# An attention-and-expert kernel whose first part runs its operations in another order, with seven squares on GpSimd

## The chip, the cores and the metric

The kernel runs on one core of a Trainium2 chip. The metric is the device time of one execution in microseconds (us); before the change the median of three runs is 1042.24 us (1042.18 to 1042.42). The core has a matrix engine (PE), a vector engine (DVE), an activation engine (ACT), GpSimd (POOL), and a queue on SyncE (SP) that issues nearly all transfers. Each engine takes its instructions strictly in the order in which the program has them, so an instruction that waits holds back all behind it on that engine.

## The reference

Random-feature attention over 8 batches, 8 heads, 576 tokens and 64 dimensions with 128 features, then a gated product with three weight matrices (512 to 1536, twice, and back):

```python
def phi(x):
    proj = np.einsum('bhsd,md->bhsm', x, omega)
    sq = np.sum(x * x, axis=-1, keepdims=True) / 2.0
    h = proj - sq
    h = h - np.max(h, axis=-1, keepdims=True)
    return np.exp(h) / np.sqrt(m)
q_p, k_p = (phi(q_s), phi(k_s))
kv = np.einsum('bhsm,bhsd->bhmd', k_p, v)
z = np.sum(k_p, axis=2)
num = np.einsum('bhsm,bhmd->bhsd', q_p, kv)
den = np.einsum('bhsm,bhm->bhs', q_p, z)[..., None] + 1e-06
...
a = x @ w_a
b = x @ w_b
return (a * b @ w_out).astype(np.float32)
```

`q_s` and `k_s` are q and k times D^-1/4. What the change touches is `sq`: the sum of squares of each key and query, which goes into the bias of the exponential.

## The kernel before

**Staging.** The work is cut into 32 units, each a batch and a pair of heads (`_b_h` in names: `natq_0_2` belongs to batch 0, head pair 2). The four pairs of batch 0 go through the functions `pair` and `tok_tail`, those of later batches through `shifted`, `divide`, `turn` and `num`. For a pair of batch 0 the steps are: project keys and queries on PE into PSUM (`ppk`, `ppq`); take maxima on DVE (`sm`, L627) and make the biases (L634, L635) with the sums of squares; exponentials on ACT (L640, 16 instructions for a pair: `hk`, `hq`); `kv` on PE (`pkv`), copied by ACT to `kvz`; three transposes of the query features on PE (`pq`), copied to `qT` by ACT or DVE; numerators and denominators on PE (`pn`, L994); the division on DVE (`rd`, `x32t`, `tails`); a transpose back (`px`, `pt`); and the result `x_0_h` in two parts, a high one that ACT casts and a low one that DVE gets by subtraction.

**Weights.** The inputs are in 64 bits. A tile `raw` of 128x512 such numbers is made into one of 32 bits by two ACT instructions (L446, L448) and a merge on DVE (L450); then a high part is cast (L396 on ACT or L398 on DVE) and a low part subtracted on DVE (L404). The tiles come in the order `raw0` = first tile of w_a (`wa0`), `raw1` = `wb0`, `raw2` = `wo0`, and so on in threes. A product of two such split numbers takes three matrix instructions.

**The blocks.** For each of 12 slices of the 1536 columns a block of 512 tokens needs 12 matrix instructions for `pa` and 12 for `pb` (L1250), a product of the two on DVE (`a`, L1258), its split into `ghl`, and 12 instructions for the output `o` (L1060). The first instruction of block 0 is `pa` of slice 0; it needs `wa0` and `x_0_0`. Blocks 2 and later use a scheme with seven products in place of eight (L1343), on sums of the weights that are made on DVE and ACT while block 1 runs. Attention units of later batches run between the blocks' instructions.

**Sums of squares.** For most units keys and queries also come in natural layout (`natk`, `natq`, at batch ends `natee`; 128x512 each). `square_sums` squares such a tile in place on ACT (L560, with the scale folded in) and sums it on DVE (L562) into `sq`. Later, POOL adds up key features (L802).

**What sets the order.** Every operation is recorded with its buffers and a cost; a planner (`Graph.plan`) plays the engines with these costs and gives one list of 5,637 operations in order of planned start. The program is emitted in that order, so each engine's and each queue's instructions stand as the list has them. Where an operation may run on more than one engine, the planner picks.

## Time and profile before

| | |
|---|---|
| median of three runs | 1042.24 us |
| the profiled execution's own time | 1041.62 us |
| its span, first to last instruction | 1039.8 us |
| PE busy | 1024.4 us (99%) |
| DVE busy | 887.3 us (85%) |
| ACT busy | 598.4 us (58%) |
| POOL busy | 114.0 us (11%) |
| bytes read and written | 255.52 MB and 57.18 MB |

A busy PE is one with a matrix instruction under way; its ends are modelled, and an instruction that is slow or held back inside the pipeline counts as busy. So what PE loses is read from its idle time, from its rate (how long twelve equal instructions take) and from the granted clock, stretch by stretch. A row of the timeline gives the start, the duration, engine, line, operation, names, shapes and count, and in brackets idle time before it and what ended that.

### The profile page before, as it was taken

The page shows a single profiled execution, that of the slowest core. Times are in us where ns is not written, and L with a number is a line of the kernel's source. Part 1 is how long each engine was busy: PE and PEld are TensorE (multiplying, and loading weights), DVE is VectorE, ACT ScalarE, POOL GpSimd, SP SyncE. Part 2 cuts the span into 40 slices and gives each one's busy share as a digit, 9 for nine tenths or more (in the row PEclk, how much of TensorE's full clock was granted, in tenths as well). Part 3 has the DMA queues.
Part 4 walks back from the last instruction along what each step waited for, and adds up shares of the span by engine and source line. Part 5 has one row for each costly group of instructions (what it writes and reads, how often), then busy time and mean ns, then how long its engine had stood idle before and what let it go on. Part 6 is the DMA issues. An engine that isn't in the chain of part 4 may idle for free.

```text
span 1039.8 us, 26266 instructions
## 1 busy us (share of the span) xinstructions
PE 1024.4 (99%) x9902; PEld 897.0 (86%) x9902; DVE 887.3 (85%) x2212; ACT 598.4 (58%) x1656; POOL 114.0 (11%) x181
## 2 busy tenths in 40 slices
PE   9899999999999999999999999999999999999998
PEld 7677777777788888988888888888899899999998
DVE  6999999899999888878887978888876579998766
ACT  8997798677665665566565656665454123332211
POOL 0032211120111111111101111111110000000000
PEclk9999999999999999999999999999999999999999
DMA  9877879989899998999989988989888888899981
GB/s 352 308 281 239 285 242 307 304 331 317 298 349 363 307 317 294 315 330 313 306 275 351 310 300 296 339 303 309 272 288 268 268 320 313 318 344 341 371 303 47
DMA packets 123665, 314.44 MB, mean 302 GB/s; under 512 B 17681, under 2 KB 40977, under 8 KB 123537
## 3 DMA queue, kind: packets, MB, share of 16 engines
q1 hardware_dynamic: 122656, 312.10, 86.5%
q8 instruction: 78, 1.28, 0.5%
q10 hardware_dynamic: 880, 0.66, 0.2%
q14 instruction: 51, 0.41, 0.1%
HBM read 255.52 MB, written 57.18 MB: 301 GB/s over the span
## 4 chain that ended last, share of the span: by engine, by line
PE 79%; DVE 8%; ACT 1%; issue 1%; DVEq 0%; ACTq 0%
PE p L1343 39%; PE o L1060 19%; PE o_P L1130 5%; PE pa L1250 3%; PE pb L1250 3%; PE pkv L849 3%; PE pm L917 2%; PE ppk L594 1%; PE p L594 1%; DVE sm L627 1%; DVE c L1353 1%; PE p L1130 1%; DVE zero L868 1%; PE ppk L574 1%; PE ppke L574 1%
## 5 line engine op out<-in xcount | busy, mean ns | idle before, releaser
L1353 DVE TENSOR_TENSOR c<-p,c 128x512 f32<-128x512 f32 (+1 forms) x336 | 207.7, 618 | 67.9 <-PE p L1343 59.4
L1060 PE MATMUL o<-wo,ghl 128*128 128x512 f32 x1008 | 258.5, 397 | 0.4 <-DVE ghl L404 0.3
L1060 PEld LDWEIGHTS o<-wo,ghl 128*128 128x128 f32 x1008 | 181.0, 188 | 39.9 <-issue 4.7
L1343 PE MATMUL p<-Sa,t 128*128 128x256 f32 x1008 | 132.6, 281 | 0.0
L1343 PEld LDWEIGHTS p<-Sa,t 128*128 128x128 f32 x1008 | 124.6, 188 | 0.4 <-issue 0.2
L802 POOL TENSOR_TENSOR z<-hk 128x256 f32<-128x256 f32 x56 | 44.5, 795 | 607.7 <-ACT hk L640 431.3
L396 ACT CAST ghl<-c 128x512 fp32r<-128x512 f32 (+1 forms) x75 | 42.5, 579 | 100.5 <-DVE c L1403 80.9
L878 ACT ACTIVATE hq<-hq,dn 128x128 f32<-128x128 f32 x224 | 71.1, 392 | 29.1 <-DVE dn L874 28.9
L868 DVE CUSTOM_DVE_ANT_0 zero<-hq,zb 128x128 bf16<-128x128 f32 x224 | 79.5, 355 | 4.9
L1250 PE MATMUL pa<-x,wa 128*128 128x512 f32 x288 | 75.9, 406 | 3.6 <-ACT wa L396 2.0
L1343 PE MATMUL p<-Sb,bq 128*128 128x256 f32 x504 | 74.1, 283 | 0.0
L1343 PE MATMUL p<-x,t 128*128 128x256 f32 x504 | 74.0, 282 | 0.0
L1250 PE MATMUL pb<-x,wb 128*128 128x512 f32 x288 | 73.3, 398 | 0.4 <-DVE a L1258 0.4
L1343 PE MATMUL p<-Sb,t 128*128 128x256 f32 x504 | 73.5, 282 | 0.0
L396 ACT COPY c<-p 128x256 f32<-128x256 f32 x84 | 31.3, 372 | 73.0 <-PE p L1343 62.3
L1343 PEld LDWEIGHTS p<-x,wa 128*128 128x128 f32 x504 | 64.9, 188 | 7.2 <-DVE c L1353 3.7
L1343 PE MATMUL p<-x,wa 128*128 128x256 f32 x504 | 68.2, 283 | 2.0 <-DVE c L1353 1.0
L1250 PEld LDWEIGHTS pa<-x,wa 128*128 128x128 f32 x288 | 53.6, 191 | 19.0 <-ACT a L396 2.2
L640 ACT ACTIVATE hq<-hq,sm 128x128 f32<-128x128 f32 x192 | 65.4, 392 | 7.4 <-DVE sm L635 6.0
L1343 PEld LDWEIGHTS p<-x,wb 128*128 128x128 f32 x504 | 64.6, 188 | 3.8 <-DVE c L1353 0.6
L1343 PE MATMUL p<-x,wb 128*128 128x256 f32 x504 | 67.7, 282 | 0.1
L1343 PEld LDWEIGHTS p<-x,t 128*128 128x128 f32 x504 | 65.8, 189 | 1.6 <-DVE c L1353 0.4
(209 smaller groups left out, 2019.6 us busy)
## 6 DMA issues: line engine op xcount, KB each, us to landing
t<-td SPq DMA_DIRECT2D x168, 512.0 KB
...
```

The costliest lines, as they stand in the source:

```text
L396: nc.scalar.copy(o(), i())
L574: nc.tensor.matmul(pps[w].ap[half, c * M:c * M + M], x()[rows, c * P + D * t:c * P + D * t + D], om.ap[rows], start=True, stop=True)
L640: g.op({"ACT": 392}, lambda e, c=c, w=w, to=to, at=at: nc.scalar.activation(to.ap[:, at + c], src[w](c), AF.Exp, scale=SC, bias=sm.ap[:, 2 ...
L802: g.op({"POOL": pool2(n)}, lambda e: nc.gpsimd.tensor_tensor(o(), a(), c(), op=ALU.add), r=r, w=w, alloc=list(al), prio=pri, deps=zload[-1 ...
L849: nc.tensor.matmul(pkv.ap[D * j + d:D * j + d + Q, 0:M], vb.ap[:, vc, d:d + Q], c(), start=(n == 0), stop=(n == 4))
L868: g.op({"DVE": 413}, lambda e, c=c, j=j, rr=rr, qc=qc: nc.vector.tensor_tensor_reduce(out=junk.ap[rr], in0=qc(), in1=zb.ap[rr, j], scale=1 ...
L878: g.op({"ACT": 392}, lambda e, c=c, src=src: nc.scalar.activation(hq.ap[:, c], src(), AF.Copy, scale=dn.ap[:, c:c + 1]), r=[sd, (dn, None) ...
L1060: nc.tensor.matmul(po.ap[:], ghl.ap[:, gi, t * P:(t + 1) * P], wo.ap[:, wi], start=(n == 0 and i == 0), stop=(n == NF - 1 and i == 2))
L1130: nc.tensor.matmul(pb.ap[:, t], A[0](ai)[:, t * P:(t + 1) * P], W[0](wi), start=begin and t == j == 0, stop=stop and t == 1 and j == 2)
L1250: nc.tensor.matmul(pb.ap[:], wt.ap[:, wi, c], xs[c].at(xi), start=(c == 0 and i == 0), stop=(c == NC4 - 1 and i == 2))
L1343: nc.tensor.matmul(pb.ap[:, half], wcol(wi, c), xc(xi, c), start=n == 0, stop=n == 5)
L1353: g.op({"DVE": dve(n)}, lambda e: nc.vector.tensor_tensor(c4.ap[:, o], pb.ap[:, half], y(), op=ALU.add), r=[*((pb, k) for k in range(half. ...
```

## The change

The planner's list is kept up to the last step, and then a fixed table rearranges it. `OTHER` gives 44 operations another engine: 7 from ACT to POOL (squares: `natq_0_1`, `natk_0_2`, `natq_0_2`, `natk_0_3`, `natq_0_3`, `natkk_1_0`, `natee_1_0`), 18 from ACT to DVE and 19 from DVE to ACT (casts and copies, of weights, of `ghl`, of `qT` and of outputs). `AFTER` puts 1,409 operations of the first 2,308 of the list behind another one. From 355 us of the profile before on, every engine's order is what it was; the buffers' places in memory are the same throughout.

A square on POOL is a plain product of the tile with itself, without the scale. The scale (SQ2) is applied by a small POOL instruction to the eight sums of each partition, after DVE's sum; the biases on DVE then wait for POOL.

```diff
+OTHER = ((61,"POOL"),(130,"POOL"),(133,"POOL"),(136,"DVE"),(139,"POOL"),(142,"POOL"),(211,"POOL"),(237,"POOL"),(259,"ACT"),(269,"DVE"),
...
+AFTER = ((6,4),(0,8),(20,16),(14,20),(23,14),(19,23),(13,19),(27,31),(35,27),(25,34),(33,36),(32,39),(48,32),(45,40),(51,45),
...
+def arranged(order):
+    for i, e in OTHER:
+        order[i].eng = {e: 0}
+    moved = {i for i, _ in AFTER}
+    follow = {}
+    for i, j in AFTER:
+        follow[j] = i
+    got = []
+    def put(i):
+        while i is not None:
+            got.append(i)
+            i = follow.pop(i, None)
+    put(follow.pop(-1, None))
+    for i in range(len(order)):
+        if i not in moved:
+            put(i)
+    return [order[i] for i in got]
...
-            g.op({"ACT": act(n * D)}, lambda e, nat=nat: nc.scalar.activation(nat.ap[:], nat.ap[:], AF.Square, scale=SQ),
-                 r=[(nat, None)], w=[(nat, None)], prio=pr, margin=0 if b < 2 else CFG["LOAD"])
-            g.op({"DVE": dve(n * D)}, lambda e, nat=nat, o=o: nc.vector.tensor_reduce(o(), nat.ap[:], axis=X, op=ALU.add),
-                 r=[(nat, None)], w=[(sq, part)], alloc=[sq] if part in (0, None) else [], prio=pr)
+            s = g.op({"ACT": act(n * D)}, lambda e, nat=nat: nc.scalar.activation(nat.ap[:], nat.ap[:], AF.Square, scale=SQ) if e == "ACT" else
+                     nc.gpsimd.tensor_tensor(nat.ap[:], nat.ap[:], nat.ap[:], op=ALU.mult),
+                     r=[(nat, None)], w=[(nat, None)], prio=pr, margin=0 if b < 2 else CFG["LOAD"])
+            def total(e, nat=nat, o=o, s=s):
+                nc.vector.tensor_reduce(o(), nat.ap[:], axis=X, op=ALU.add)
+                if "POOL" in s.eng:
+                    nc.gpsimd.tensor_scalar(o(), o(), SQ2, 0.0, op0=ALU.mult, op1=ALU.add)
+            g.op({"DVE": dve(n * D)}, total, r=[(nat, None)], w=[(sq, part)], alloc=[sq] if part in (0, None) else [], prio=pr)
...
-    order = g.plan()
+    order = arranged(g.plan())
```

Line numbers in the changed kernel are higher by 25 in the helpers and by 30 behind `square_sums`. Three places show how the rows move.

First, SP's queue of loads, from its thirteenth transfer on. Before:

```order
L407 DMA X_0_30_171<-in_kqt_dram 128x1024
L407 DMA natk_0_3_173<-in_kqn_dram 128x512
L407 DMA natq_0_3_175<-in_kqn_dram 128x512
L407 DMA v_0_3_177<-in_vx_dram 128x660
L407 DMA Xe_1_0_202<-in_kqtt_dram 128x512
L407 DMA Xk_1_0_204<-in_kqt_dram 128x512
L407 DMA X_1_0_206<-in_kqt_dram 128x1024
L407 DMA raw0_216<-in_wab_dram 128x512
L407 DMA raw1_218<-in_wab_dram 128x512
```

Now:

```order
L432 DMA natq_0_3_168<-in_kqn_dram 128x512
L432 DMA Xe_1_0_191<-in_kqtt_dram 128x512
L432 DMA raw1_197<-in_wab_dram 128x512
L432 DMA raw0_199<-in_wab_dram 128x512
L432 DMA v_0_3_201<-in_vx_dram 128x660
L432 DMA raw5_327<-in_wout_dram 128x512
L432 DMA natkk_1_0_382<-in_kqn_dram 128x512
L432 DMA X_0_30_384<-in_kqt_dram 128x1024
```

The first two weight tiles stand earlier (`raw0` sixteenth instead of twentieth, `raw1` fifteenth instead of twenty-first), and `X_0_30`, the keys and queries of head pair 3, later (twentieth instead of thirteenth).

Second, ACT and DVE where the fourth head pair of batch 0 ends and block 0 begins. ACT before:

```order
L396 COPY qT_0_3_740<-pq_0_31_784 128x384
L446 ACTIVATE raw1_218<-raw1_218 128x512
L448 ACTIVATE raw1_218<-raw1_218 128x512
L448 ACTIVATE raw0_216<-raw0_216 128x512
L396 COPY kvz_0_3_791<-pkv_0_3_790 128x132
L446 ACTIVATE raw0_216<-raw0_216 128x512
L396 CAST x_0_2_829<-px_0_2_828 128x512
L396 COPY xts0_571<-pt_0_2_835 128x64
L446 ACTIVATE raw2_223<-raw2_223 128x512
L448 ACTIVATE raw2_223<-raw2_223 128x512
L448 ACTIVATE raw3_267<-raw3_267 128x512
L396 CAST wa0_878<-raw0_216 128x512
```

ACT now:

```order
L471 ACTIVATE raw4_523<-raw4_523 128x512
L473 ACTIVATE raw4_523<-raw4_523 128x512
L473 ACTIVATE raw3_517<-raw3_517 128x512
L421 COPY qT_0_3_738<-pq_0_31_777 128x384
L421 COPY kvz_0_3_782<-pkv_0_3_781 128x132
L473 ACTIVATE raw2_519<-raw2_519 128x512
L421 COPY qT_0_3_738<-pq_0_32_805 128x384
L421 CAST x_0_2_842<-px_0_2_841 128x512
```

DVE before:

```order
L450 SCALAR_TENSOR_TENSOR raw1_218<-raw1_218 128x512
L398 COPY qT_0_3_740<-pq_0_32_838 128x384
L404 TENSOR_TENSOR x_0_2_829<-px_0_2_828,x_0_2_829 128x512
L450 SCALAR_TENSOR_TENSOR raw0_216<-raw0_216 128x512
L450 SCALAR_TENSOR_TENSOR raw2_223<-raw2_223 128x512
L398 CAST wb0_880<-raw1_218 128x512
L999 TENSOR_SCALAR rd_0_31_865<-pn_0_31_864 128x5
L404 TENSOR_TENSOR wa0_878<-raw0_216,wa0_878 128x512
L404 TENSOR_TENSOR wb0_880<-raw1_218,wb0_880 128x512
```

DVE now:

```order
L423 CAST wa0_835<-raw0_199 128x512
L1032 TENSOR_TENSOR x32t_0_2_754<-pn_0_21_765,rd_0_21_766 128x4x64
L1036 TENSOR_SCALAR tails_0_2_731<-pn_0_20_752,rd_0_20_753 64x64
L1032 TENSOR_TENSOR x32t_0_2_754<-pn_0_20_752,rd_0_20_753 128x4x64
L423 COPY qT_0_3_738<-pq_0_30_737 128x384
L429 TENSOR_TENSOR wb0_810<-raw1_197,wb0_810 128x512
L429 TENSOR_TENSOR wa0_835<-raw0_199,wa0_835 128x512
L475 SCALAR_TENSOR_TENSOR raw4_523<-raw4_523 128x512
L1029 TENSOR_SCALAR rd_0_30_859<-pn_0_30_858 128x5
L1029 TENSOR_SCALAR rd_0_31_875<-pn_0_31_874 128x5
L429 TENSOR_TENSOR x_0_2_842<-px_0_2_841,x_0_2_842 128x512
```

ACT's conversions of `raw0` and `raw1` have moved ahead, between the exponentials of head pairs 2 and 3; the high parts of `wa0` and `wb0` are both cast by DVE, and the low parts follow right behind the first copy to `qT_0_3`.

Third, POOL's first compute instructions, which are all new (before, POOL does nothing but clear tiles until it adds up key features, L802):

```order
L586 TENSOR_TENSOR natq_0_2_154<-natq_0_2_154 128x512
L586 TENSOR_TENSOR natq_0_1_152<-natq_0_1_152 128x512
L592 TENSOR_SCALAR sq_0_1_302<-sq_0_1_302 128x8
L586 TENSOR_TENSOR natk_0_3_158<-natk_0_3_158 128x512
L586 TENSOR_TENSOR natk_0_2_160<-natk_0_2_160 128x512
L586 TENSOR_TENSOR natq_0_3_168<-natq_0_3_168 128x512
L1015 MEMSET tails_0_0_469 64x128
L592 TENSOR_SCALAR sq_0_3_471<-sq_0_3_471 128x8
L592 TENSOR_SCALAR sq_0_2_474<-sq_0_2_474 128x8 x2
L592 TENSOR_SCALAR sq_0_3_471<-sq_0_3_471 128x8
L586 TENSOR_TENSOR natkk_1_0_382<-natkk_1_0_382 128x512
L586 TENSOR_TENSOR natee_1_0_386<-natee_1_0_386 128x512
```

The squares of pair 3 and pair 2 stand between the small scalings, which wait for DVE's sums.

More of the change, by code (lines that the diff above doesn't have):

```diff
@@ L42 @@
 CFG = dict(PORT=0.5, EDF=("DVE", "ACT", "POOL"), STEP=15000, LOOK=60000, NOISE=(200, 600), CHOSEN=((858009,0,387055,152612,0,0,0,715321,0,0,680034,0,0,0,0,780129,689749,0,892332,0,0,84647,0,0,0,0,0,0,0,0,0,0,0,0,0,0,0,0,0,0,0,0,0,0,0,0,0,0,0,0,0,0,0,0,0,0,0,0,0,0,0,0,0,0,0,0,0,0,0,0),), ZS=800, ZB=(300, 1600, 3600), ZD=(300, 1600, 3100), HQ=(1100, 2600, 3600), BACK2=(300, 1100, 2600), TW=(), XL=["v0", "v1", "Xt0", "ht2", "hq0"], OWR=["raw0", "raw1"], ONE=((7, 1),), SAFE=500, OWN=16, OWNU=(), HOLD=1000, TG=1, G4=4, WAIT=150, RAW=600, FAST=(0, 1, 2, 3), JOIN0=False, WARM=8, HROOM=["w0", "u1", "w1", "u2", "w2", "u3"], H=3, TURN=(7,), BACK=1500, AT=2, GATES=(-4, -1, 2, 5), SQPE=4, MARGIN=1200, LOAD=1100, SUMS=1000, NATS=(1, 2, 3), CONV=(28000, 2600))
+OTHER = ((61,"POOL"),(130,"POOL"),(133,"POOL"),(136,"DVE"),(139,"POOL"),(142,"POOL"),(211,"POOL"),(237,"POOL"),(259,"ACT"),(269,"DVE"),(297,"ACT"),(352,"ACT"),(355,"DVE"),(423,"DVE"),(447,"ACT"),(449,"ACT"),(475,"ACT"),(494,"ACT"),(560,"ACT"),(562,"ACT"),(638,"ACT"),(674,"ACT"),(708,"ACT"),(720,"ACT"),(740,"DVE"),(794,"DVE"),(868,"DVE"),(976,"DVE"),(1006,"DVE"),(1142,"DVE"),(1152,"DVE"),(1168,"ACT"),(1224,"DVE"),(1255,"ACT"),(1331,"DVE"),(1403,"ACT"),(1498,"ACT"),(1597,"DVE"),(1679,"DVE"),(1848,"ACT"),(1892,"DVE"),(1950,"ACT"),(2035,"DVE"),(2049,"DVE"),)
```

1 line of the change is left out of this document (added).

## The prediction

> **What bounds the kernel now.** I read the page first, then PE's waits, the windows, and the timeline around the longest wait.
>
> ```profile
> PE 1024.4 (99%) x9902; PEld 897.0 (86%) x9902; DVE 887.3 (85%) x2212; ACT 598.4 (58%) x1656; POOL 114.0 (11%) x181
> 50.00:150.00 100.00, 98.59 (x847) 75.27 (x847) 98.93 (x258) 86.63 (x228) 23.55 (x30) 1.00 0.80 273
> 300.00:450.00 150.00, 149.00 (x1554) 132.48 (x1552) 127.35 (x339) 87.53 (x255) 17.99 (x30) 1.00 0.93 325
> ```
>
> The last two rows are windows: length, busy time of PE, weight load, DVE, ACT and POOL, granted clock, share and rate of the DMA engines. PE is the bound: busy 99% of the span. Another order can win only where PE idles or runs slowly before it becomes the old order again. Windows of 5 us show where that is:
>
> ```profile
> 0.00:5.00 5.00, 4.00 (x36) 1.82 (x40) 0.11 (x1) 2.12 (x3) 0.99 (x10) 1.00 0.57 182
> 5.00:10.00 5.00, 5.00 (x100) 4.54 (x92) 4.07 (x9) 3.61 (x11) 0.00 (x0) 1.00 0.97 343
> 10.00:15.00 5.00, 5.00 (x116) 4.20 (x115) 4.82 (x14) 4.97 (x18) 0.00 (x0) 1.00 1.04 408
> 15.00:20.00 5.00, 4.39 (x93) 3.39 (x94) 3.28 (x12) 5.00 (x20) 0.00 (x0) 1.00 1.05 410
> 20.00:25.00 5.00, 4.57 (x116) 3.84 (x114) 4.90 (x12) 5.00 (x17) 0.20 (x1) 1.00 1.03 412
> 25.00:30.00 5.00, 4.27 (x116) 3.68 (x109) 4.62 (x16) 4.82 (x19) 0.00 (x0) 1.00 1.04 402
> 30.00:35.00 5.00, 4.74 (x95) 4.01 (x95) 4.51 (x15) 5.00 (x19) 0.20 (x1) 1.00 1.02 408
> 35.00:40.00 5.00, 2.69 (x58) 2.25 (x54) 4.46 (x8) 5.00 (x12) 0.20 (x1) 1.00 0.87 342
> 40.00:45.00 5.00, 4.49 (x12) 3.24 (x13) 4.88 (x14) 5.00 (x10) 0.00 (x0) 0.66 0.57 209
> ```
>
> From 10 to 45 us ACT is full, DVE is not (3.28 of 5 at 15), POOL does nothing, and PE waits. From 40 to 45 the granted clock is 0.66. PE's waits name the work, first from 37 to 52 us, then from 52 to 450:
>
> ```profile
> PE pa L1250 <- ACT wa L396: 2.0, 1, 2.0
> PE pn L994 <- ACT kvz L396: 0.8, 1, 0.8
> PE pa L1250 <- ACT a L396: 0.7, 1, 0.7
> ```
>
> ```profile
> PE p L1343 <- ACT hk L396: 0.8, 1, 0.8
> PE pa L1250 <- ACT a L396: 0.7, 1, 0.7
> PE pb L1250 <- DVE a L1258: 0.4, 1, 0.4
> PE o L1060 <- DVE ghl L404: 0.3, 1, 0.3
> ```
>
> So 3.5 us of idle PE in 15 us and, with two rows of 0.2 left out, 2.6 us in the next 400. Before 37 us the longest wait that is not the program's start is this one, two more of 0.5 and 0.4 behind it:
>
> ```profile
> PE px L1013 <- DVE x32t L1002: 0.7, 1, 0.7
> ```
>
> The first stretch on the timeline of PE, and one of full rate:
>
> ```profile
> 37.12 1.39 PE L994 MATMUL pn<-kvz,qT 128*64 128x66 f32 x40 [0.82 <-ACT kvz L396]
> 40.51 3.95 PE L1250 MATMUL pa<-x,wa 128*128 128x512 f32 x9 [2.00 <-ACT wa L396]
> 44.27 2.50 PE L1250 MATMUL pb<-x,wb 128*128 128x512 f32 x9
> 50.71 1.53 PE L1250 MATMUL pa<-x,wa 128*128 128x512 f32 x5 [0.69 <-ACT a L396]
> 138.09 2.92 PE L1250 MATMUL pa<-x,wa 128*128 128x512 f32 x12
> ```
>
> Nine instructions take 3.76 us from 40.51 to 44.27; at full rate twelve take 2.76 (138.09 to 140.85), so nine 2.07. The low clock costs 1.7 us there, and 0.2 in the next nine.
>
> **The change part by part.** I follow one milestone: the start of `pa` of slice 1, at 50.71. Behind it PE hardly waits, so what is gained there stays, if the others keep up.
>
> (1) *The squares leave ACT.*
>
> ```profile
> 19.65 0.78 ACT L560 ACTIVATE natk<-natk 128x512 f32<-128x512 f32 x1
> 20.17 0.78 ACT L560 ACTIVATE natq<-natq 128x512 f32<-128x512 f32 x1
> 34.88 0.93 ACT L446 ACTIVATE raw<-raw 128x512 f32<-128x512 f32 x1
> 35.46 1.46 ACT L448 ACTIVATE raw<-raw 128x512 int32<-128x512 uint32 x2
> 36.57 0.50 ACT L396 COPY kvz<-pkv 128x132 f32<-128x132 f32 x1
> ```
>
> Starts lie 0.52 us apart for squares and 0.55 for conversions: that is what one holds of ACT. All seven squares stand ahead of `kvz_0_3` (36.57), the copy for which `pn` of pair 3 waits: 7 x 0.52 = 3.6. A third of `qT_0_1` goes to DVE, 0.4 more. Ahead of `kvz_0_3` come instead four conversions more than before (both of `raw4`, one of `raw3`, the second of `raw0`): 4 x 0.55 = 2.2. Net, ACT is there 1.8 earlier.
>
> (2) *DVE takes over as second bound.*
>
> ```profile
> 32.53 0.55 DVE L398 COPY qT<-pq 128x384 f32<-128x384 f32 x1
> 38.77 1.33 DVE L450 SCALAR_TENSOR_TENSOR raw<-raw 128x512 int32<-128x512 int32 x2
> 40.02 0.42 DVE L398 CAST wb<-raw 128x512 fp32r<-128x512 f32 x1
> 40.49 0.69 DVE L404 TENSOR_TENSOR wa<-raw,wa 128x512 fp32r<-128x512 f32 x1
> ```
>
> Ahead of the first copy to `qT_0_3` (32.53), which `pn` needs too, now stand two merges and two sums of squares at about 0.6, two casts at 0.35, and the divisions of pair 2, 2.3: 5.4 us more. In the windows from 5 to 35 us DVE is busy 26.2 of 30, and its instructions start a little ahead of the last one's end, so some 4.4 of idle time lie there to be filled: the copy comes between 33.5, all of it used, and 37.9, none. I take 35.4, a little nearer to the first, since the merges and sums wait for loads and for POOL alone, not for PE. `pn` starts 0.6 behind it, at 36.0 instead of 37.12, and ACT is there by then: **-1.1** (bounds -3 and +1).
>
> (3) *The wait for wa.* Right behind that copy DVE makes the low parts of `wb0` and `wa0`, whose raw tiles are converted long before: 0.5 + 0.6 + 0.7 = 1.8 behind the copy's start, while `pn` ends 2.0 behind it (0.6 + 1.4). The wait of 2.0 shrinks to about 0.3: **-1.7** (bounds -2.0 and 0).
>
> (4) *The clock.* The one drop of the granted clock inside the program follows the one idle stretch of 2.0 us; waits of 0.7 and 0.8 did not bring it. With 0.3 it should not come: **-1.9** (bounds -1.9 and 0).
>
> (5) *What is late next.* `px_0_3` stands fourth after `pa`'s begin; DVE divides its input behind the low parts, a merge, a subtraction and four small ones, 4.5 behind the copy; PE arrives at 2.3 + 3 x 0.69 = 4.4: with a semaphore's delay **+0.3** (0 to +2). The wait at 50.71 goes, as `wa1` and `x_0_3` have less ahead of them on both engines: **-0.8** (-0.8 to 0).
>
> (6) *The loads.* By the windows' rates 0.9 MB have moved by 5 us, 2.6 by 10, 4.7 by 15, 6.7 by 20. In the new order 4.9 and 5.4 MB end with `raw1` and `raw0` (15.5 and 17 us; 6.9 and 7.4 before), and 7.0 with `X_0_30`, near 21 us. PE took it up at 22.84:
>
> ```profile
> 22.84 0.32 PE L574 MATMUL ppk<-om,X 64*64 64x128 f32 x1
> ```
>
> That costs nothing unless PE runs ahead there by over 1 us.
>
> (7) *The squares on POOL.*
>
> ```profile
> L802 POOL TENSOR_TENSOR z<-hk x56: 724/742/1093, 52.7 to 771.5; 128x256 f32<-128x256 f32 x56
> L802 POOL TENSOR_TENSOR zs<-z x56: 450/476/1143, 53.7 to 772.7; 128x128 f32<-128x128 f32 x56
> 15.49 0.17 DVE L635 SCALAR_TENSOR_TENSOR sm<-sq,sm 128x8 f32<-128x8 f32 x1
> 69.20 1.23 DVE L404 TENSOR_TENSOR wo<-raw,wo 128x512 fp32r<-128x512 f32 x1
> L802 POOLq MODIFY_POOL_CONFIG x2: 4/4/4, 36.2 to 36.2; - x2
> ```
>
> Minimum, median and longest, in ns: 128 columns more cost 266 by the medians, so 512 take 742 + 2 x 266 = 1.27 us (estimate; bounds 1.0 and 2.3, twice the longest). The first tile is the sixth transfer, 1.6 MB: by the rates 7 us, and with a transfer's delay I take 8.9. Four squares in a row end at 14.0; the scaling that stands between the second and the third waits for DVE's sum and makes that about 15. DVE asks for the fourth when it has made pair 1's biases, at 15.66: hidden, by little. The other scalings stand off the path. The price lies on DVE: its subtraction at 69.20 took 1.23, not 0.69, with POOL at work beside it. In the first 35 us five such instructions may meet a square, 5 x 0.54 = 2.7 at most, much of it in idle time: **+0.4** (0 to +2.7).
>
> (8) *The order from 52 to 450 us.* Here only in-order queues count. With each operation at its kind's spacing I compared work ahead of PE's instruction and ahead of its producer, old and new. The producers that end the waits of the table above gain 1 to 3 us of lead (`wa6`, `ghl` of slices 4 and 11, the first sums of block 2); near 337 to 375 some lose about 1. I take **-1.0** of the 2.6 (bounds -2.6 and +3). DVE's work ahead at 300 us differs by only 0.3, ACT's is less. After 450 nothing changes.
>
> Sum: -1.1 - 1.7 - 1.9 + 0.3 - 0.8 + 0.4 - 1.0 = -5.8. The profiled execution took 1041.62 us, 1.8 around its span of 1039.8, which the order does not touch: 1035.8. It stands 0.6 below the median of the runs, so **1036.4**.
>
> **Rivals.** (a) *More*: PE's waits before 37 us, 1.6, go too, `px_0_3` waits for nothing, and all of (8) comes: another 1.6 + 0.3 + 1.6, about 1033. For it: ACT was full there. Against: so is DVE now.
>
> (b) *The clock still drops*: DVE late by 1 us keeps a wait ahead of `pa`: 1.9 and 1.0 come back, 1039.3.
>
> (c) *DVE is already the bound*: busy 98.93 of 100 from 50 to 150. If that were full, a PE that starts 5 us earlier runs into it, and with 0.3 less work ahead at 300 us all is lost: 1042. Against: an instruction of 0.69 starts 0.60 to 0.65 after the last (38.77, two in 1.33), so 12% of busy is overlap, and PE waited for DVE only 0.9 of 400 us.
>
> (d) *Slower: POOL's queue is late.* The fourth square ends at about 10 + 4X for a square of X; from X = 1.5 on, DVE stands at the sum of `natk_0_2`, with the divisions of pair 0 and the maxima of pair 2 behind it, and PE waits for these. Each 0.1 more costs 0.4; at 3.5 it is 8, so 1036.4 + 8 = 1044.4. Against: no L802 row comes near. The same happens if POOL's first operation has to wait for its code: before, POOL was prepared for L802 at 36.2 us, 16 us ahead of its first use, so no row prices it. The Trainium skill (GPSIMD Engine Reference, Instruction dispatch) has a first call of a newly loaded routine cost some 6 us without a trace row; begun at 1.6 us that ends ahead of 8.9, begun at the call it would come to 1036.4 + 6 = 1042.4.
>
> **How the numbers follow.** Forecast 0.45, with 1034.5 to 1038.5 as its own range; (a) 0.18; (b) 0.17; (c), or gains and late queues in balance, 0.12; (d) 0.08. A measurement here tells 0.2%, 2.1 us, from no change. Faster: 0.45 + 0.18 + 0.17 = 0.80; same 0.12; slower 0.08. The range reaches over (a) and (b) and stops ahead of (c): 1031.5 to 1040.9, the lower end for bounds that add up below (a).
>
> **What would show it.** Right: `pn` of pair 3 near 36.0, `pa` behind it with under 0.7 of idle time, granted clock 1.00 from 35 to 45, `pa` of slice 1 near 45.5, the same lead at 150 and 450 us; squares on POOL of 1.2 to 1.5 us, each over before DVE's sum asks for it. Wrong: a clock under 1 there, DVE idle for POOL at 15 to 17 us, or a lead that shrinks between 50 and 300.

## The result, and the profile after

The changed kernel takes 1055.02 us (1053.06 to 1056.23, four runs) beside 1042.26 us (1042.18 to 1042.42): a ratio of 1.012, 95% interval 1.0103 to 1.0138. It is 12.8 us slower. The forecast was 1036.4.

The profiled execution has a span of 1053.6 us, 13.8 longer. By 50 us it has gained nearly what was forecast, though not step by step as forecast (below). Windows of 5 us of the changed kernel, with the columns as in the prediction:

```profile
35.00:40.00 5.00, 4.50 (x91) 3.90 (x92) 4.92 (x17) 5.00 (x11) 0.20 (x1) 1.00 0.77 263
40.00:45.00 5.00, 5.00 (x52) 3.86 (x51) 4.91 (x13) 4.84 (x11) 0.00 (x0) 1.00 0.99 378
45.00:50.00 5.00, 5.00 (x24) 4.01 (x22) 4.96 (x12) 5.00 (x14) 0.81 (x1) 1.00 1.03 411
```

PE is busy 14.5 of 15 us, 12.2 before, and the granted clock is 1.00. On the timeline of PE the block begins without a wait, and slice 1 begins at 46.60 instead of 50.71:

```profile
37.98 1.39 PE L1024 MATMUL pn<-kvz,qT 128*64 128x66 f32 x40
39.30 1.66 PE L1280 MATMUL pa<-x,wa 128*128 128x512 f32 x6
...
46.60 2.89 PE L1280 MATMUL pa<-x,wa 128*128 128x512 f32 x12
```

The loss lies behind it. PE's waits from 60 to 460 us, the five longest in total:

```profile
PE pb L1280 <- DVE a L1288: 3.3, 3, 1.7
PE p L1373 <- DVE c L1383: 1.8, 2, 1.4
PE o L1090 <- DVE ghl L429: 1.5, 3, 0.9
PE o L1090 <- ACT osb L421: 1.3, 1, 1.3
PE p L1373 <- ACT c L421: 0.9, 2, 0.5
```

Before, all waits there came to 2.6 us; these five are 8.8, and PE is busy for 387.4 of these 400 us, 397.1 before. Around the longest of them, windows of the changed kernel show PE at 3.27 of 5, and the clock falls behind it:

```profile
170.00:175.00 5.00, 3.27 (x23) 1.90 (x16) 4.93 (x12) 3.55 (x11) 2.71 (x4) 0.90 0.16 64
175.00:180.00 5.00, 5.00 (x65) 3.55 (x68) 4.64 (x19) 2.23 (x4) 0.00 (x0) 0.76 0.51 129
```

A low clock as the prediction found it at 41 us comes here instead, once: by these two windows it costs some 1.5 us (0.10 of 3.27 and 0.24 of 5.00). The DMA share of 0.16 shows a second thing: few transfers are under way there.

The orders differ, so the times of single instructions say little. For the comparisons below I gave every operation of PE (and of DVE) the spacing that its kind reaches in the fastest tenth of the kernel before, added these up, and asked when each kernel had done as much work as the kernel before at a given time. The lead in us (minus: behind), for the runs told below; the column is the time in the kernel before. Where the orders differ most the count depends on what is taken as one kind: with kinds by names and shapes some entries at 200 and 300 us move by up to 5 us, those at 180 and from 360 on by at most 0.5.

```
                            60     100    140    180    200    300    360    450   1000
changed kernel        PE   4.3     3.4    1.0   -3.1   -4.8   -7.3  -11.9  -12.1  -13.9
                      DVE  2.0     0.8   -3.0   -6.9   -4.9  -10.9  -11.2
e1 early              PE   5.0     1.1    1.2    1.1    1.1    1.1    0.9    0.7   -1.2
e2 late               PE  -0.5    -0.6   -2.3   -4.7   -7.1   -8.8  -13.4  -13.4  -13.5
                      DVE -0.5    -3.2   -6.3   -8.4   -7.9  -12.4  -12.8
e3 half               PE   5.0     4.0    1.4   -1.2   -9.7   -9.4   -9.9  -10.1  -12.1
e18 late from 180     PE  -0.5    -0.5   -0.5   -0.5   -3.6   -6.1  -10.6  -10.6  -10.8
e10 before, bunched   PE  -0.2    -0.6   -1.9   -2.6   -2.6   -4.6   -4.8   -4.9   -4.6
e11 new, no adds      PE   4.2     4.5    4.9    4.8    2.5    2.0   -1.8   -2.0   -3.8
e12 before, no adds   PE  -0.7    -0.1    0.6    0.6    0.6    1.8    1.8    1.9    1.7
e14 new, small dn     PE   4.4     4.7    3.2    2.0   -0.4   -0.9   -5.1   -5.4   -7.2
e16 early, no adds    PE   4.2     1.9    3.1    3.2    3.1    4.5    4.3    4.2    2.5
e17 early, addresses  PE   4.8     1.4    1.6    1.6    1.6    1.7    1.7    1.7    1.7
```

So the 13.8 us (13.9 by this count) are 4.3 gained by 60 us, 16.4 lost from there to 450, and 1.8 lost between 450 and 1000, where the order of every engine is the same as before.

### The profile page after: what moved, and what is told of

It reads as the page before. It is cut to its first block, busy times and chain, and to the rows that moved or that the text cites. A ratio compares the mean times of both kernels' runs of the same rounds, so it can differ in the third digit from the quotient of the medians.

```text
span 1053.6 us, 26259 instructions
## 1 busy us (share of the span) xinstructions
PE 1030.6 (98%) x9902; PEld 900.1 (85%) x9902; DVE 894.7 (85%) x2211; ACT 595.6 (57%) x1650; POOL 123.9 (12%) x195
## 4 chain that ended last, share of the span: by engine, by line
PE 70%; DVE 16%; ACT 6%; DMA 5%; issue 2%; SPq 1%; POOL 0%; DVEq 0%; ACTq 0%; POOLq 0%
PE p L1373 38%; PE o L1090 16%; PE o_P L1160 4%; PE pkv L879 2%; DVE zero L898 2%; DVE sm L657 2%; PE pm L947 2%; PE ppk L624 1%; PE p L624 1%; DVE raw L475 1%; DVE c L1383 1%; ACT hq L908 1%; DVE sq L590 1%; ACT hk L670 1%; ACT hq L670 1%
## 5 line engine op out<-in xcount | busy, mean ns | idle before, releaser
L1090 PE MATMUL o<-wo,ghl 128*128 128x512 f32 x1008 | 265.1, 398 | 3.0 <-DVE ghl L429 1.5
L832 POOL TENSOR_TENSOR z<-hk 128x256 f32<-128x256 f32 x56 | 46.9, 838 | 617.3 <-ACT hk L670 455.5
L908 ACT ACTIVATE hq<-hq,dn 128x128 f32<-128x128 f32 x224 | 72.7, 393 | 34.0 <-DVE dn L904 33.8
L898 DVE CUSTOM_DVE_ANT_0 zero<-hq,zb 128x128 bf16<-128x128 f32 x224 | 81.8, 365 | 9.1 <-DMA zb<-zdr 2.4
L1280 PE MATMUL pb<-x,wb 128*128 128x512 f32 x288 | 79.0, 400 | 3.3 <-DVE a L1288 3.3
L1280 PE MATMUL pa<-x,wa 128*128 128x512 f32 x288 | 79.2, 402 | 0.6 <-DVE wa L429 0.6
L670 ACT ACTIVATE hk<-hk,sm 128x128 f32<-128x128 f32 x184 | 63.6, 393 | 9.5 <-DVE sm L665 4.6
L1280 PEld LDWEIGHTS pb<-x,wb 128*128 128x128 f32 x288 | 53.0, 188 | 17.9 <-DVE a L1288 5.0
```

What stands on the lines that cost most here:

```text
L670: g.op({"ACT": 392}, lambda e, c=c, w=w, to=to, at=at: nc.scalar.activation(to.ap[:, at + c], src[w](c), AF.Exp, scale=SC, bias=sm.ap[:, 2 ...
L832: g.op({"POOL": pool2(n)}, lambda e: nc.gpsimd.tensor_tensor(o(), a(), c(), op=ALU.add), r=r, w=w, alloc=list(al), prio=pri, deps=zload[-1 ...
L898: g.op({"DVE": 413}, lambda e, c=c, j=j, rr=rr, qc=qc: nc.vector.tensor_tensor_reduce(out=junk.ap[rr], in0=qc(), in1=zb.ap[rr, j], scale=1 ...
L908: g.op({"ACT": 392}, lambda e, c=c, src=src: nc.scalar.activation(hq.ap[:, c], src(), AF.Copy, scale=dn.ap[:, c:c + 1]), r=[sd, (dn, None) ...
L1090: nc.tensor.matmul(po.ap[:], ghl.ap[:, gi, t * P:(t + 1) * P], wo.ap[:, wi], start=(n == 0 and i == 0), stop=(n == NF - 1 and i == 2))
L1280: nc.tensor.matmul(pb.ap[:], wt.ap[:, wi, c], xs[c].at(xi), start=(c == 0 and i == 0), stop=(c == NC4 - 1 and i == 2))
```

## The experiments

**Which part of the order loses (e1 to e3, e18).** The list of the changed kernel up to a place and the rest in the order of before, or the reverse; an operation has the engine of the list that it stands in. The first fence is e1, with 395 operations of the new list, about 60 us (e3 takes 1,240, about 200 us); the second is e2 (e18 takes 1,146).

```diff
-    return [order[i] for i in got]
+    early = set(got[:395])
+    for i, e in OTHER:
+        if i in early:
+            order[i].eng = {e: 0}
+    return [order[i] for i in got[:395]] + [order[i] for i in range(len(order)) if i not in early]
```

```diff
-    return [order[i] for i in got]
+    for i, e in OTHER:
+        if i >= 395:
+            order[i].eng = {e: 0}
+    return order[:395] + [order[i] for i in got if i >= 395]
```

> This kernel takes the first 395 operations of the new order (up to about 60 us, with their engines, all seven squares on POOL among them), and behind them everything in the order of before. By work done on PE the changed kernel led by 4.3 us at 60 us and trailed by 11.9 at 380. Theory M (the new order of the operations from 60 to 355 us is itself the loss): the lead of 4.3 stays, 1042.3 - 4.3 = 1038.0 us, 1036.5 to 1039.5. Theory L (the lead is what is lost: DVE is full from 60 to 300 us, and a PE that arrives early runs into it and upsets the queues): 1042 or more, up to 1055. Theory P (the squares on POOL upset DVE and the loads in the first 35 us, and the loss only shows later): 1055, as in the changed kernel.

> This kernel takes the first 395 operations in the order of before, no square on POOL, and behind them everything in the new order. Theory M: the loss of 4.3 + 11.9 + the 1.9 that it still loses behind 380 us comes without the gain: 1042.3 + 16 to 18 = 1058 to 1060 us. Theory L: without a lead there is nothing to lose: 1042, 1041 to 1044. Theory P: 1042 as well.

> This kernel takes the first 1240 operations of the new order (up to about 200 us), and behind them the order of before. In the changed kernel PE had lost 9.2 us of its lead by 200 us (from +4.3 to -4.8) and lost 7.1 more by 380. Theory M: 1042.3 + 4.8 = 1047 us, 1045 to 1049. Theory L: the order of before behind a late PE loses nothing more, or even makes some of it good: 1042 to 1047. If it comes out at 1055, the loss of the second half is not in its order either.

e1: 1042.79 us, ratio 1.0008 (0.9999 to 1.0018). e2: 1054.67, 1.0124 (1.0107 to 1.0141). e3: 1053.44, 1.0115 (1.01 to 1.013). The order from 60 us on costs 12 us by itself, without any lead ahead of it (e2). That is theory M, though 3 us under its range. But e1 doesn't keep the lead of 5.0 either: 1.1 are left at 100 us, in the order of before. That part is theory L. By the table, 3.9 lost in e1 from 60 to 100 us and 12.9 lost in e2 from 60 to 450 come to 16.8, near the 16.4 of the changed kernel. PE's waits in e1 from 55 to 85 us, and the window of the kernel before in which they fall:

```profile
PE ppq L606 <- ACT k L423: 1.3, 1, 1.3
PE o L1092 <- ACT xts L423: 0.6, 1, 0.6
PE pb L1282 <- DVE a L1290: 0.3, 1, 0.3
```

```profile
60.00:80.00 20.00, 20.00 (x236) 15.39 (x229) 19.86 (x45) 19.51 (x48) 4.72 (x6) 1.00 0.73 255
```

PE waits for two copies on ACT, which is busy 19.51 of 20 us there, as DVE is. By work done ACT is 1.8 us behind the kernel before at 60 us and DVE 2.7 ahead: the early order had put PE forward by 5.0, and the engines that serve it by less or not at all.

e3 lies above the ranges of both theories. It loses 8.5 between 180 and 200 us (from 1.2 behind to 9.7), at the seam of the two lists. One wait there is for a weight that is loaded back from memory:

```profile
PE o L1092 <- DMA wo<-wod: 4.4, 1, 4.4
PE pb L1282 <- DVE a L1290: 1.7, 1, 1.7
PE o L1092 <- ACT osb L423: 1.3, 1, 1.3
```

A seam can so cost by itself, and the parts don't simply add up. e18 asks the same of the second half alone:

> The first 1146 operations (up to about 180 us) in the order of before, and behind them the new order with its engines. In the late kernel PE lost 4.2 us between 60 and 180 and 8.7 between 180 and 360. Theory F (the order from 180 us on is bad by itself): 1042.3 + 7 to 10 = 1049 to 1052 us. Theory G (it loses there because DVE came late out of the first half, 8.4 us at 180, and the queues behind it): 1042 to 1045.

1052.23 us, ratio 1.0089 (1.0074 to 1.0104): theory F, 0.2 above its range. The order from 180 us on loses 10 us without a late first half ahead of it. This run has a seam too, at 180 us, and what the seam alone costs was not tried.

**The squares (e4).** Seven entries of `OTHER` are skipped, so that ACT makes all squares.

```diff
     for i, e in OTHER:
-        order[i].eng = {e: 0}
+        if e != "POOL":
+            order[i].eng = {e: 0}
```

> The changed kernel with the seven squares back on ACT, at the same places of the order; everything else as in the change. My own step of the prediction: seven squares hold ACT for 0.52 us each, 3.6 in all, most of them ahead of pair 3, so the early gain of 4.3 shrinks to between 1 and 3, and the total, if the rest is as in the changed kernel, is 1055 + 1.5 to 3.5 = 1056.5 to 1058.5. Theory P: without POOL beside DVE the loss goes: 1045 or below. Theory L: a smaller lead, a smaller loss: 1050 to 1055.

1062.69 us, 1.0193 (1.0173 to 1.0213): 7.7 us worse than the changed kernel, where I had 1.5 to 3.5, and PE is 3.1 us behind at 60 us instead of 4.3 ahead. The new order counts on the squares being elsewhere: PE has one wait of 5.3 us for a copy that now stands behind them on ACT, and the clock is halved behind it. PE's longest wait up to 60 us, and a window:

```profile
PE pn L1025 <- ACT kvz L422: 5.3, 1, 5.3
```

```profile
20.00:25.00 5.00, 3.82 (x55) 3.26 (x55) 0.51 (x4) 4.66 (x18) 0.00 (x0) 0.50 0.37 143
```

In the changed kernel a square on POOL takes 1.04 us, and the first begins at 8.61, with no wait for code that the trace would show. The group of three of the seven, and the first two on the timeline of POOL:

```profile
L586 POOL TENSOR_TENSOR natq<-natq 128x512 f32<-128x512 f32 x3 | 3.1, 1039 | 7.4 <-DMA natq<-in_kqn_dram 7.4
```

```profile
8.61 2.04 POOL L586 TENSOR_TENSOR natq<-natq 128x512 f32<-128x512 f32 x2 [7.38 <-DMA natq<-in_kqn_dram]
```

So theory P of e1 to e4 (the squares do the harm) falls: e1 has the squares on POOL and is not slow, e2 has none and is.

**Three causes that were not it (e5 to e8).** On the late kernel: the sums of keys make no trip through memory (e5), the sums of products wait for nobody (e6), no engine changes (e8); and both first edits on the kernel before, as a control (e7).

```diff
-        g.op({"SP": 330}, dma(lambda: zd, lambda: zx.ap[0:8]), ...
+        g.op({"SP": 330}, dma(lambda: zd, lambda: om.ap[0:8, 0:32]), ...
-        ... dma(lambda: flat(zb), lambda: zd.rearrange("c r -> (c r)").partition_broadcast(P)) ...
+        ... dma(lambda: flat(zb), lambda: idn[0:2].rearrange("c r -> (c r)").partition_broadcast(P)) ...
...
-                    out=junk.ap[rr], in0=qc(), in1=zb.ap[rr, j], scale=1.0, ...
+                    out=junk.ap[rr], in0=ident.ap[rr], in1=om.ap[rr], scale=1.0, ...
...
-        if i >= 395:
-            order[i].eng = {e: 0}
```

> The late kernel (order of before up to 60 us, new order behind it, 1054.7 us), in which the sums of keys no longer make their trip through memory: the small write to zdr takes a constant tile in place of zx, so that SP's queue doesn't wait for zx, and the broadcast zb is loaded from a constant input. The order of every engine is kept; the denominators are then wrong, the work is the same. Theory T (trips through memory: the new order leaves the loads of zb and of the turned queries less time, SP's queue stands at zx for 26 us between 60 and 200 instead of 15, and the chain of waits runs through such transfers): 4 to 9 us of the 12.4 come back, 1046 to 1051. Theory D (DVE is full there, and the new order puts other work ahead of what PE needs from it): no change, 1053 to 1056. Theory E (the 37 operations that change between ACT and DVE): no change.

> The late kernel, in which the nine sums of products of a unit on DVE (dn) read two constant tiles in place of the exponentials hq and the broadcast zb. They stay where they are in DVE's order and take as long, but DVE waits there neither for ACT nor for a transfer. Their start-to-start times stand 11.7 us above their best between 60 and 200 us and 10.4 between 200 and 360, against 8.2 and 6.2 in the kernel before. Theory T, and a theory L (DVE stands in step behind ACT's exponentials in waits too short for the table): 4 to 10 us come back, 1045 to 1051. Theory D: no change beyond 2 us, 1052 to 1055. Theory E: no change.

> The kernel before with both of these edits, as a control: PE waits there for only 2.6 us between 52 and 450 us and the chain of waits there is PE alone. All theories: 1040 to 1043 us. If it gains 4 us or more, the two edits make the work itself cheaper and the two runs above say nothing on the order.

> The late kernel without the 37 engine changes between ACT and DVE: every operation runs on the engine of before, in the new order. Theory E: most of the 12.4 us comes back, 1042 to 1046. Theories T and D: within 3 us of 1054.7; a little worse if the changes were made to fit the order.

e5: 1054.19 us, ratio 1.0113 (1.0093 to 1.0133), 0.5 less than the late kernel. SP's queue then stood for DVE all the same. SP's longest wait from 150 to 210 us in e2 and in e5:

```profile
SPq L433 <- DVE zx L860: 11.5, 3, 8.4
```

```profile
SPq L433 <- DVE sq L591: 10.9, 2, 8.5
```

What the transfer at the queue's head waits for has changed its name and not its length: DVE is late, and the loads with it. e6: 1052.50, ratio 1.0103 (1.0083 to 1.0122), 2.2 less: neither wait is where the 12 us are. e7, the control: 1041.36, ratio 0.9992 (0.9982 to 1.0002), as expected. e8: 1067.38, ratio 1.0236 (1.0216 to 1.0256), 12.7 worse than the late kernel, and more than any theory had. (By the table `OTHER` 31 changes between ACT and DVE lie behind the 395th operation, not 37.) The engine changes are part of this order and not its harm.

**Neighbours on DVE (e9, e10).** By work done DVE falls behind first: in e2 by 3.2 us at 100 and 6.3 at 140, PE by 0.6 and 2.3. The first 120 sums of products `dn` (L868, L898 in the changed kernel), those of the first 2,308 operations, take 40.1 us in the kernel before, each counted to the start of the next instruction, 48.6 in e2 and 50.3 in the changed kernel. Several things lengthen them. Rows of DVE and of POOL in the late kernel:

```profile
77.76 0.28 DVE L899 CUSTOM_DVE_ANT_0 zero<-hq,zb 128x128 bf16<-128x128 f32 x1
...
78.08 0.29 DVE L899 CUSTOM_DVE_ANT_0 zero<-hq,zb 128x128 bf16<-128x128 f32 x1
...
78.53 0.29 DVE L899 CUSTOM_DVE_ANT_0 zero<-hq,zb 128x128 bf16<-128x128 f32 x1
...
78.97 0.29 DVE L899 CUSTOM_DVE_ANT_0 zero<-hq,zb 128x128 bf16<-128x128 f32 x1
...
79.79 0.84 DVE L899 CUSTOM_DVE_ANT_0 zero<-hq,zb 128x128 bf16<-128x128 f32 x1
```

```profile
79.62 0.86 POOL L833 TENSOR_TENSOR z<-hk 128x256 f32<-128x256 f32 x1 [6.47 <-ACT hk L671]
```

One that is followed by something else holds DVE for 0.21 (median). The pairs shown stand 0.32, 0.45 and 0.44 apart, and I took 0.45 for the price of a neighbour. It is two prices. The same pairs in e6, where the sums read constants and so wait for neither ACT nor a transfer:

```profile
77.86 0.29 DVE L899 CUSTOM_DVE_ANT_0 zero<-ident,om 128x128 bf16<-128x128 f32 x1
...
78.19 0.29 DVE L899 CUSTOM_DVE_ANT_0 zero<-ident,om 128x128 bf16<-128x128 f32 x1
...
78.53 0.29 DVE L899 CUSTOM_DVE_ANT_0 zero<-ident,om 128x128 bf16<-128x128 f32 x1
...
78.86 0.29 DVE L899 CUSTOM_DVE_ANT_0 zero<-ident,om 128x128 bf16<-128x128 f32 x1
```

All three now stand 0.33 or 0.34 apart, so the neighbour costs 0.12 us, and the other 0.11 belongs to what the sum waits for. The trace of e12, with no additions beside them, separates the two cleanly: a sum behind a sum starts 433 to 446 ns after it where it has two semaphores to wait for (33 pairs), 311 to 337 where it has one (7), 258 to 304 where it has none (3). The median of 447 in the expectations is of pairs that are mostly of the first kind. Of the 48 pairs of the changed kernel 38 have fewer than two semaphores. Last, the sum beside an addition on POOL takes 0.84. In the first 2,308 operations of the kernel before 6 of 120 are followed by another, in the changed kernel 48.

e9 pulls 34 other DVE instructions up between two such sums; e10 does the reverse to the kernel before, and moves 60 sums back to right ahead of the next; the fence is e9, and in e10 the last line is `moved(g.plan())`.

```diff
+MOVE = ((x, y), ...)        # operation x is put right ahead of operation y
+def moved(order):
+    by = {o.n: o for o in order}
+    for x, y in MOVE:
+        order.remove(by[x])
+        order.insert(order.index(by[y]), by[x])
+    return order
-    order = arranged(g.plan())
+    order = moved(arranged(g.plan()))
```

> The changed kernel, in which 34 other DVE instructions are pulled up by a few places so that they stand between two sums of products (dn) that stood side by side: of 120 such sums in the first 2,308 operations 14 instead of 48 then follow another directly (6 in the kernel before). Theory N (neighbours): a dn behind a dn starts 447 ns after it (median), another instruction behind a dn 211 ns, so 42 more such pairs cost DVE 42 x 0.236 = 9.9 us, DVE is the engine that falls behind first (by work done it is 8 us late at 180 us in the late kernel, PE 4.7), and PE loses them in turn. Then 34 x 0.236 = 8.0 us come back: 1047 us, 1046 to 1050. Theory P (POOL's additions of key features run beside dn and make it twice as long): no change, 1053 to 1056. Theory W (DVE has to wait for ACT and PE in the new order, whatever stands beside what): no change, or worse.

> The kernel before, with nothing changed but 60 of the sums of products moved back on DVE to right ahead of the next one: 62 of 120 then follow another directly, instead of 6. Theory N: DVE loses 56 x 0.236 = 13.2 us at most between 60 and 375 us, and PE loses that less what slack DVE had: 1047 to 1055. Theories P and W: within 2 us of 1042.3, since each sum is moved by only a few places.

e10: 1047.09 us, ratio 1.0047 (1.003 to 1.0063), at the lower edge of theory N: 56 more pairs cost 4.7 us, not 13. At 0.12 a pair 6.7 would have been expected. e9: 1062.59, 1.0197 (1.0181 to 1.0212), 7.6 worse where 8 better were expected (at 0.12 a pair it would have been 4). From 60 to 180 us it loses as much as the changed kernel (7.1 and 7.4), so parting the pairs gave nothing back there; then 7.5 at once. ACT's timeline in e9, and PE's longest wait:

```profile
193.41 0.39 ACT L682 ACTIVATE hq<-hq,sm 128x128 f32<-128x128 f32 x1
200.62 1.28 ACT L920 ACTIVATE hq<-hq,dn 128x128 f32<-128x128 f32 x4 [6.82 <-DVE dn L916]
201.80 0.60 ACT L433 CAST ghl<-a 128x512 fp32r<-128x512 f32 x1
202.31 0.57 ACT L433 COPY osb<-o 128x512 f32<-128x512 f32 x1
```

```profile
PE o L1102 <- ACT osb L433: 4.9, 1, 4.9
```

ACT stands for 6.8 us at the scaling of the queries, for which the last sum on DVE is late, and two instructions that PE needs stand behind it. Instructions that were moved for DVE's sake have made a chain DVE, ACT, PE longer. The same wait grows in the changed kernel; how much of PE's loss there hangs on it was not tried. ACT's, from 60 to 380 us, before and after:

```profile
ACT hq L878 <- DVE dn L874: 9.0, 7, 3.8
```

```profile
ACT hq L908 <- DVE dn L904: 14.3, 7, 3.7
```

**POOL's additions, and DVE's time (e11, e12, e14, e15).** The additions of key features become clears of the same tiles (e11, e12); or each sum on DVE takes 16 columns of 128 (e14, e15).

```diff
-            ... lambda e: nc.gpsimd.tensor_tensor(o(), a(), c(), op=ALU.add) ...
+            ... lambda e: nc.gpsimd.memset(o(), 1.0) ...
...
-                    out=junk.ap[rr], in0=qc(), in1=zb.ap[rr, j], scale=1.0, ...
+                    out=junk.ap[rr, 0:16], in0=qc()[:, 0:16], in1=zb.ap[rr, j, 0:16], scale=1.0, ...
```

> The changed kernel, in which POOL's 168 additions of key features (L832) are replaced by clears of the same tiles, so that nearly nothing runs beside DVE on POOL behind 50 us (the sums of keys are left out, the denominators are then wrong). Theory P: dn beside an addition takes 640 ns, alone 282; in the middle 60 of 120 are beside one, which is 8 to 10 us: 1045 to 1048 us, and the control without the additions in the order of before gains no more than 2. Theory N: dn behind dn is as slow as before; up to 4 us from shorter instructions, 1051 to 1055.

> The kernel before with POOL's additions replaced by clears in the same way. PE waits there for 2.6 us in 400: all theories 1040 to 1042.5 us. A larger gain would say that the additions cost both orders alike, and the run above has to be read as the difference of the two.

> The changed kernel, in which each sum of products (dn, 280 of them on DVE) takes only 16 of its 128 columns (the denominators are then wrong); every instruction stays where it is. A dn takes 282 ns alone and 640 beside POOL's additions; I expect 130 to 200 of the shorter one, so DVE gains 12 to 25 us between 60 and 375 us. Theory D: the loss of 16 us behind 60 us goes and the lead of 4.3 stays for the most part: 1037 to 1041. Theory PE (the order is bad for PE and the loads as well): 1046 to 1052.

> The kernel before with the same shorter sums. PE waits for 2.6 us between 52 and 450: 1038.5 to 1041.5 us by every theory (without the additions it was 1039.4). It is the measure for the run above.

Without the additions the new order takes 1045.08 us, ratio 1.0025 (1.0015 to 1.0034), 9.9 less; the order of before 1039.35, 0.9974 (0.9964 to 0.9983), 3.0 less. Theory P gave the first of these numbers. The control gained more than any theory had, and so, as its expectation says, the two runs have to be read by their difference: with the additions the new order is 12.8 us behind the old one, without them 5.7, so 7.1 us hang on the additions. The groups of DVE from 60 to 360 us, changed kernel and e11:

```profile
L898 DVE CUSTOM_DVE_ANT_0 zero<-hq,zb 128x128 bf16<-128x128 f32 x88 | 35.9, 408 | 5.2 <-DMA zb<-zdr 2.4 <-ACT hq L670 0.6
L475 DVE SCALAR_TENSOR_TENSOR raw<-raw 128x512 int32<-128x512 int32 x26 | 18.6, 722 | 0.8 <-ACT raw L471 0.8
```

```profile
L898 DVE CUSTOM_DVE_ANT_0 zero<-hq,zb 128x128 bf16<-128x128 f32 x93 | 26.7, 287 | 4.9 <-ACT hq L670 2.1 <-DMA zb<-zdr 0.9
L475 DVE SCALAR_TENSOR_TENSOR raw<-raw 128x512 int32<-128x512 int32 x26 | 17.6, 684 | 0.1
```

A sum takes 287 ns instead of 408, and PE keeps its whole lead up to 180 us (4.8). Yet the additions lengthen the sums in the order of before too: the first 120 take 43.1 us there and 33.8 in e12, 47.4 in the changed kernel and 34.3 in e11, so 9.3 us against 13.1. The new order lengthens them by only 3.8 us more; most of the 9.3 costs PE nothing in the order of before, where 3.0 us come back.

Nor do e11 and e12 take away only what runs beside DVE. A clear reads nothing: in the changed kernel POOL waits 455.5 us in total for ACT's `hk` ahead of these additions, in e11 for none of it, and what follows on POOL's results can come earlier. e14 leaves the additions and only makes the sums shorter, to 257 ns in the mean from 60 to 360 us. It takes 1051.42 (1048.71 to 1052.94, three runs), ratio 1.0086 (1.0066 to 1.0107): 3.6 less than the changed kernel, and 6.7 less by the profiled executions (spans of 1046.9 and 1053.6). That is in the range of theory PE. e15: 1039.90, 0.9981 (0.9971 to 0.9991), 2.3 less. Theory D, that DVE's time is all, does not hold: the shorter sums give back a third (by the medians) to two thirds (by the profiled executions) of what leaving out the additions does, and even without the additions the new order is 5.7 us behind the old one without them. It loses 6.6 between 180 and 360 us (from 4.8 ahead to 1.8 behind in e11), and 1.8 behind 450.

**Whether the early gain can be kept (e13, e16, e17).** On the early kernel: twelve casts from DVE to ACT (e13), no additions (e16).

```diff
-        if i in early:
+        if i in early or (e == "ACT" and i < 1300):
             order[i].eng = {e: 0}
```

> The early kernel (new order up to about 60 us, then the order of before), with twelve casts between 60 and 200 us (wo3, wa4, wb4, wa5, wa6, wo6, wb7, wa8 and the high parts of four ghl) moved from DVE to ACT, as the change has them. In the early kernel PE led by 5.0 us at 60 us, by 1.1 at 100; DVE led by 2.7 and 1.1. Theory D (DVE is full from 60 to 180 us in the order of before too, so a lead of PE lasts only as far as DVE's): 12 x 0.42 = 5 us less on DVE, the lead stays between 3 and 5: 1038 to 1041 us, against 1042.8. Theory O (the lead is lost at the seam of the two orders): no change, 1042 to 1043.5. If ACT then comes late, 1044 or more.

> The early kernel with POOL's additions replaced by clears, as in e12, which took 1039.4 us in the order of before. Theory D: with DVE relieved the lead of 5.0 at 60 us lasts: 1039.4 - 4 to 5, plus the 1.9 that the early kernel lost behind 400 us: 1036 to 1038. Theory O: 1039.4 to 1041, as without the early part.

e13: 1044.32 us, 1.0024 (1.0014 to 1.0034), as expected if ACT comes late: the lead is gone at 80 us (-0.1). e16: 1038.86, 0.9971 (0.9961 to 0.998), 0.5 below e12, between the two theories: 2.9 of 4.2 us are lost by 80 us, and the rest lasts. Both engines that serve PE are full there (the window above), and relief of DVE at ACT's cost made the kernel slower.

In e16 as in e1 some 1.8 us go behind 450 us, in instructions that are the same in the same order. A place in memory gets its address at its first use. The places of the buffers are the same in both kernels, as I wrote ahead of the prediction, but the first uses are not in the same order, so tiles can lie at other addresses; no trace shows an address. e17 asks for each place once in the order of before, ahead of all else:

```diff
-    order = arranged(g.plan())
+    planned = g.plan()
+    seen = set()
+    order = arranged(planned)
...
+        for o in planned:
+            for b in o.alloc:
+                if b.slot not in seen:
+                    seen.add(b.slot)
+                    (ps if b.ring in PS else sp).tile(b.shape, b.dtype, tag=b.slot, name="first" + b.name)
         for o in order:
```

> The early kernel with one difference: ahead of everything each place in memory is asked for once in the order of before, so that all 1,793 tiles have the addresses that they have in the kernel before; the order of every engine is that of the early kernel. Theory A (addresses): the 1.9 us that the early kernel loses between 400 and 1000 us in the same instructions go, PE needs 599.4 us for them as in the kernel before and not 601.4, and the kernel takes 1042.8 - 1.9 = 1040.9 us, 1040 to 1041.8. Theory B (something that the early order leaves behind, in a queue or in the code): 601.4 and 1042.8 as before.

1040.88 us (1040.15 to 1041.59, 11 runs), ratio 0.9987 (0.9978 to 0.9995): theory A, to the tenth. From 400 to 1000 us of the kernel before PE takes 599.4 us for the same instructions, 601.4 in e1, 599.4 in e17. The group of the output's instructions from 600 to 700 us, in e1 and in e17:

```profile
L1092 PE MATMUL o<-wo,ghl 128*128 128x512 f32 x132 | 34.1, 398 | 0.0
```

```profile
L1092 PE MATMUL o<-wo,ghl 128*128 128x512 f32 x132 | 33.9, 397 | 0.0
```

No wait shows it, only the length of the instructions. The table of leads has the same split: the runs that begin in the new order (changed kernel, e1, e3, e11, e14, e16) lose 1.7 to 2.0 us between 450 and 1000, those that begin in the old one (e2, e10, e12, e18) 0.3 at most, and e17 nothing. e17, which leaves nothing out, is 1.9 us faster than e1 and 1.2 faster than the kernel before (1042.05 in the same runs); that is less than the 0.2% by which I judged, and its interval is clear of 1. The changed kernel itself was not run with the old addresses, so what they cost it ahead of 450 us is not known; e17 leads e1 by 0.5 at 180 us.

## Why the prediction was wrong

The sum was right up to 60 us: 4.3 us gained by work done, where terms (1) to (7) come to -4.8. Its steps were so only in part, and that the sum agrees is partly luck: (2) missed by 2.0 us, and from the begin of `pn` to slice 1 (13.59 us before, 8.62 now) 0.9 more was gained than (3) to (5) had.

- (1), ACT 1.8 earlier at `kvz_0_3`: not seen. The copy began at 36.54, 36.57 before, and nothing on the path was gained by it.
- (2), `pn` of pair 3 at 36.0: wrong by 2.0. It began at 37.98, 0.9 later than before. The copy to `qT` came at 37.06, close to the 37.9 that stood for a DVE whose idle time takes nothing up; I had chosen the other side of the middle. PE's waits ahead of this `pn` grew too, to 1.4 for a `kvz` of ACT and 1.1 for an `x32t` of DVE; before, the longest there was 0.7.
- (3), the wait for `wa`: right. The wait of 2.0 is gone, not shrunk to 0.3, because the low parts of `wb0` and `wa0` were over at 38.80 and the late `pn` ended at 39.37.
- (4), the clock, came as forecast (1.00), but its -1.9 was too much. The same wait of 2.0 at the same place was followed, in the window from 40 to 45 us, by 0.66 to 0.71 in the kernel before, e10 and e2, and by 1.00 in the seven other runs that begin in the old order (e5 to e8, e12, e15, e18). At the full clock slice 1 begins 9.4 us behind `pa` (50.92 and 41.55 in e18), and PE waits 0.7 for `tails` (DVE) in between; in the kernel before it begins 10.2 behind. So the low clock cost 0.8 there, and only in some executions. Rows of e18 and that window:

```profile
41.55 2.61 PE L1281 MATMUL pa<-x,wa 128*128 128x512 f32 x9 [2.04 <-ACT wa L422]
50.92 3.41 PE L1281 MATMUL pa<-x,wa 128*128 128x512 f32 x12 [0.39 <-ACT a L422]
40.00:45.00 5.00, 3.45 (x14) 2.54 (x15) 4.94 (x12) 5.00 (x10) 0.00 (x0) 1.00 0.36 113
```
- (5) was right in the whole: `px_0_3` began 2.2 behind `pa` without a wait, the wait at 50.71 is gone, and slice 1 began 4.1 us earlier; I had 5.2.
- (6) was right: `X_0_30` was taken up at 25.25, 2.4 later than before, and no wait names it.
- (7) was right in size: 1.04 us for a square (estimate 1.27, bounds 1.0 and 2.3), all of them over before DVE asks; rival (d) did not happen. The price of the squares on DVE, +0.4, no run shows by itself. On the code that the Trainium skill (GPSIMD Engine Reference, Instruction dispatch) says a first call has to load: the first square took 1.04 us as the others, begun as soon as its data had landed, so nothing was paid at the call. POOL was prepared for it at 1.2 us, 7.4 ahead; whether a load ran in between can't be seen.
- (8), the order from 52 to 450 us, is the step that failed: -1.0, bounds -2.6 and +3, measured +16.4. I had compared work ahead in the queues with one fixed spacing for each kind of operation. Two terms were not in it: what stands behind a sum on its own engine (0.21 us or 0.33; e10 gives 4.7 us for 56 more pairs), and what runs beside it on another (282 ns alone, 543 in the median of those that overlap an addition). I used the second in (7), for a row of 1.23 us, and not here. By these the 42 more pairs cost DVE some 5 us (42 x 0.12, an estimate) and the additions 3.8 us more than before. What they cost the kernel is another matter: leaving the additions out is worth 9.9 us in the new order and 3.0 in the old, so I read the larger part as slack: what the old order hid, the new one has to pay. No run shows that by itself. And I took the gain of some producers for a gain of PE, while ACT's wait for `dn` grew from 9.0 to 14.3 us and PE's waits from 2.6 to 8.8 in the five longest alone.
- Rival (c) had the engine: DVE falls behind first in the late kernel. I set it at 0.12 with the argument that 12% of its busy time is overlap and PE waited for it only 0.9 us; e1 shows that a lead of 5.0 leaves 1.1 in the order of before, for ACT's sake as well as DVE's. Its price of "all is lost" was still too low, as it had no room for an order that is worse than the old one.
- No term stood for the 1.8 us behind 450 us. "After 450 nothing changes" was wrong: the addresses do (shown by e17 on the early kernel, which loses as much).

What stays open: of the 12.8 us by which the new order is slower, 7.1 hang on the additions on POOL and 5.7 stay without them (e11 beside e12). Why shorter sums alone give back so much less than leaving out the additions is not settled. The merges on DVE (722 ns against 684) and the low parts of `ghl` (711 against 679) are lengthened beside POOL too, and the clears don't wait for ACT; neither was tried by itself. What stays without the additions is lost between 180 and 360 us (6.6 in e11). e18 shows that this part of the order loses by itself, and no single wait was shown to cause it.
